# RMS norm of batches 1 to 8 on one compact tile, its inverse root spread by fp32r halves, and x reloaded into its own slot

## The chip, the cores and the metric

The kernel runs on one core of one Trainium2 chip. A core has TensorE (PE in the profile; PEld is its weight load), VectorE (DVE), ScalarE (ACT), GpSimd (POOL) and SyncE (SP, which only issues DMAs here). Each engine works through its own list of instructions in order and waits on semaphores for the others. The metric is the device time of one execution in microseconds, as the median of several runs.

## The reference

Three layers in a row: a linear attention with an RMS norm over each head's 64 values, a maximum of three projections with an output projection, and a second FFN with a squared ReLU.

```python
# q, k, v: 8 batches, 8 heads, 576 rows, 64 columns
kv = np.einsum('bhsd,bhse->bhde', k, v)
out = np.einsum('bhsd,bhde->bhse', q, kv)
rms = np.sqrt(np.mean(out * out, axis=-1, keepdims=True) + 1e-06)
x = out / rms * g_norm                  # -> 4608 tokens x 512
h = np.maximum(np.maximum(x @ w1, x @ w2), x @ w3)   # 512 -> 768
x = h @ w_out                                        # 768 -> 512
r = np.maximum(x @ w_in, 0.0)                        # 512 -> 2048
out = (s * (r * r) + b) @ moe2_w_out                 # 2048 -> 512
```

## The kernel before

**Tiles.** A token block is 512 tokens. Each batch has 576 rows: 512 make block 0 to 7, and the 64 left over of all batches make block 8. The attention output `o` of a batch is kept with features on the partitions: four tiles of 128 x 512, one for each pair of heads p (two heads of 64 features). So the mean of the squares of a head is a sum over 64 partitions, which TensorE makes by a product with a constant matrix, and the factor 1/rms must be on all those partitions again before VectorE can multiply.

**Number form.** Products are in fp32r, a reduced form of fp32. An fp32 value is kept as two of them: a high part (ScalarE copies and rounds, `hi_part`) and a low part (a subtraction, `lo_part`). `mm3` (lines 160 to 163) makes one product as three: hi x hi, hi x lo, lo x hi. Some small products are in plain fp32; the profile shows each of those as two MATMUL instructions.

**Stages.** For j = 0 to 4, `g1_part` makes 18 groups (3 projections x 6 blocks of 128) of 12 products each from x, and `g2_mm` then makes 4 output blocks of 18 products from h. These two fill TensorE; the attention of later batches is woven between their groups. x of batches 0 and 1 stays on chip. From batch 2 on the normed o is stored to DRAM (`xd`) and, for batches 2 to 4, loaded again before its turn. Batches 5 to 8 are read from `xd` in a later stage. From about 380 us on there is no attention left.

**Order.** Every piece of work is a `job` with a place in time, an engine, a cost and the names that it reads, writes and allocates. `arrange` (lines 71 to 131) goes through the jobs with these costs and writes a fixed order for each engine: an engine takes the earliest planned job that is ready. So a job that gets other costs or another place moves its neighbours too. The engines then follow that order, whatever the real durations are.

**Three ways to norm.** `PLAIN` = 2 divides the batches.

- Batch 0: compact, two head pairs at a time. `msc_mm` multiplies the squares with `means` (128 x 32) in fp32 and puts pair p on partitions 32p to 32p + 31 of one PSUM tile, each by a tile of its own of the array (128 rows, 32 columns). `rsqrt_c` makes Ln, Exp, Square on ScalarE and two steps on VectorE for all of them at once, with the result in `uc`. `bc_mm` spreads a pair of rows over 128 partitions by a product of `spread` with `uc`, 32 rows and 128 columns of the array, in fp32. `normed` multiplies o with it.
- Batch 1: the same with all four head pairs in one tile (`WIDE` = 4).
- Batches 2 to 8: each head pair alone on a whole tile. The square is split in two fp32r halves (`sq_hi` on VectorE or ScalarE, `sq_lo` on GpSimd), `ms_mm` makes two products of 128 x 128 x 512 with `ones`, whose result stands on all partitions already, and `rsqrt` and `newton` make three steps on ScalarE and three on VectorE for each pair. Batch 8 squares `o_rem`, the left-over rows.

**Buffers.** PSUM tile `o` (two banks, one buffer) holds the attention output of two head pairs, and in batches 0 and 1 also `bc`. PSUM tile `ms` (one bank) holds the left-over rows of the attention product and the means. `xh` and `xl` hold x of one block, one buffer each. `x_back` (line 533) loads x of a batch by head pair into small tiles, of which there are two: the first two quarters are loaded early, the last two when the first have been read. It is issued on SP's queue, as nearly all DMAs are.

Of the kernel before, what the change touches and what calls it, by code (L numbers as in the profile page):

```python
# [30 lines left out]
def attention_max_ffn_relu2_ffn(ctx: ExitStack, tc, q, k, v, g_norm, w1, w2, w3, wo, wi, w2o, s, b, out):  # L31
# [462 lines left out]

    def normed(bb, p):
        o = st["o", bb, p]
        stt(out=o, in0=o, scalar=g_sb, in1=st["bc", p // 2][p % 2], op0=ALU.mult, op1=ALU.mult)

    def rsqrt(bb, p, n):
        if n == 0:  # L500
            st["y", p] = at_.tile([P, N], F32, tag="y", name=f"y_{bb}_{p}")
            act(out=st["y", p], in_=st["ms", p], func=AF.Ln, bias=eps)
        elif n == 1:
            act(out=st["y", p], in_=st["y", p], func=AF.Exp, scale=-0.5)
        else:
            st["u", p] = at_.tile([P, N], F32, tag="u", name=f"u_{bb}_{p}")
            act(out=st["u", p], in_=st["y", p], func=AF.Square)

    def newton(bb, p, n):
        y, u = st["y", p], st["u", p]  # L510
        if n == 0:
            stt(out=u, in0=st["ms", p], scalar=EPS, in1=u, op0=ALU.add, op1=ALU.mult)
        elif n == 1:
            stt(out=u, in0=u, scalar=-3.0, in1=y, op0=ALU.add, op1=ALU.mult)
        else:
            o = st["o", bb, p]
            stt(out=o, in0=o, scalar=g_sb, in1=u, op0=ALU.mult, op1=ALU.mult)
# [1066 lines left out]
```

## Time and profile before

| | us |
|---|---|
| median of 3 runs | 1358.96 (1358.86 to 1359.13) |
| profiled execution | 1358.27 |
| its span, first to last instruction | 1356.5 |
| TensorE busy | 1336.8 |
| VectorE busy | 982.4 |
| ScalarE busy | 788.0 |
| GpSimd busy | 68.1 |

The profile shows one execution. An instruction's row has its start, its duration, the line of the kernel and the tiles. Durations on TensorE overlap: a product is in flight for 0.39 us while the next one starts 0.23 us behind it. What a product costs is therefore the distance from one start to the next. Where an engine stood idle before an instruction, brackets say how long and what it waited for.

### The profile page before, as it was taken

What the parts mean: (1) busy time and instruction counts of PE and PEld (TensorE: products, weight loads), DVE (VectorE), ACT (ScalarE), POOL (GpSimd) and SP (SyncE); (2) the same over time, 40 slices, a digit from 0 to 9 for tenths busy, and PEclk for the clock granted to TensorE, in tenths of its full rate; (3) what the DMA queues carried; (4) which work ended last, traced back from release to release, by engine and by line L of the source; (5) the groups of instructions that cost most, each with busy time, mean ns of one, the idle gap of its engine ahead of it and who ended that gap; (6) DMA issues with size and microseconds to landing.
All of it is one profiled execution on the core that took longest, in us unless ns stands there. A gap on an engine that the chain in (4) does not pass through costs nothing.

```text
span 1356.5 us, 19727 instructions
## 1 busy us (share of the span) xinstructions
PE 1336.8 (99%) x6948; PEld 1102.0 (81%) x6948; DVE 982.4 (72%) x1671; ACT 788.0 (58%) x1399; POOL 68.1 (5%) x58
## 2 busy tenths in 40 slices
PE   7999999999999999999999999999999999999998
PEld 4777777778888888878888889888888888888888
DVE  4994666767658885477647768658888888888875
ACT  6873555556435453165546567567775656566565
POOL 0001212123110000000000000000000000000000
PEclk9999999999999999999999999999999999999999
DMA  9988988753527638575535645436584464554531
GB/s 267 298 181 210 221 215 224 209 157 95 152 87 249 240 117 267 205 244 184 177 149 196 238 174 169 172 139 223 194 307 151 142 211 142 178 164 138 182 113 48
DMA packets 241010, 251.81 MB, mean 186 GB/s; under 512 B 119184, under 2 KB 177552, under 8 KB 238736
## 3 DMA queue, kind: packets, MB, share of 16 engines
q1 hardware_dynamic: 240752, 250.31, 59.9%
q8 instruction: 54, 0.88, 0.3%
q14 instruction: 44, 0.36, 0.1%
q10 hardware_dynamic: 160, 0.26, 0.1%
HBM read 149.85 MB, written 100.66 MB: 185 GB/s over the span
## 4 chain that ended last, share of the span: by engine, by line
PE 95%; DVE 2%; DMA 1%; SPq 1%; ACT 1%; issue 0%; ACTq 0%; DVEq 0%
PE ps_a L999 15%; PE zs_a L1153 14%; PE g L161 10%; PE g L163 9%; PE g L162 9%; PE ps_b L999 7%; PE fp_a L1392 7%; PE zs_b L1153 7%; PE zs_c L1153 4%; PE ps_c L999 4%; PE fp_b L1392 4%; PE fp_c L1392 2%; PE kvor L348 1%; PE ops L417 1%; PE ms L456 1%; DMA vrem<-in_v_dram 1%
## 5 line engine op out<-in xcount | busy, mean ns | idle before, releaser
L290 ACT ACTIVATE zx<-z 128x512 fp32r<-128x512 f32 (+1 forms) x280 | 158.4, 586 | 122.6 <-PE zs_a L1153 37.8
L1153 PE MATMUL zs_a<-zx,w_q 128*128 128x512 f32 (+1 forms) x960 | 210.9, 368 | 1.0 <-DVE zx L293 1.0
L293 DVE TENSOR_TENSOR zx<-z,zx 128x512 fp32r<-128x512 f32 (+1 forms) x280 | 171.3, 634 | 53.6 <-ACT zx L290 50.2
L999 PE MATMUL ps_a<-x_q,w_q 128*128 128x512 f32 (+1 forms) x960 | 206.0, 368 | 0.0
L1153 PEld LDWEIGHTS zs_a<-zx,w_q 128*128 128x128 f32 x960 | 168.2, 189 | 31.2 <-DVE zx L293 1.2
L999 PEld LDWEIGHTS ps_a<-x_q,w_q 128*128 128x128 f32 x960 | 167.8, 189 | 29.9
L161 PE MATMUL g<-xh,w_w 128*128 128x512 f32 x360 | 142.6, 396 | 0.0
L163 PE MATMUL g<-xh,w_w 128*128 128x512 f32 x360 | 140.4, 390 | 0.7 <-DVE w_w L293 0.7
L162 PE MATMUL g<-xl,w_w 128*128 128x512 f32 x360 | 140.3, 390 | 0.0
L1153 PE MATMUL zs_b<-zx,w_q 128*128 128x512 f32 (+1 forms) x480 | 108.5, 368 | 1.9 <-DVE zx L293 1.9
L999 PE MATMUL ps_b<-x_q,w_q 128*128 128x512 f32 (+1 forms) x480 | 105.1, 368 | 0.0
L1153 PEld LDWEIGHTS zs_b<-zx,w_q 128*128 128x128 f32 x480 | 84.5, 188 | 17.3 <-DVE zx L293 2.3
L999 PEld LDWEIGHTS ps_b<-x_q,w_q 128*128 128x128 f32 x480 | 84.2, 189 | 15.0
L161 PEld LDWEIGHTS g<-xh,w_w 128*128 128x128 f32 x360 | 67.5, 188 | 15.6 <-issue 0.8
L163 PEld LDWEIGHTS g<-xh,w_w 128*128 128x128 f32 x360 | 67.6, 188 | 15.5 <-DVE w_w L293 1.1
L162 PEld LDWEIGHTS g<-xl,w_w 128*128 128x128 f32 x360 | 67.6, 188 | 13.7 <-DVE xl L293 0.3
L576 DVE TENSOR_TENSOR h<-g,h 128x512 f32<-128x512 f32 x60 | 41.5, 691 | 38.5 <-PE g L163 37.3
L1028 ACT ACTIVATE cs<-cs 128x512 f32<-128x512 f32 (+1 forms) x60 | 35.1, 586 | 53.5 <-DVE cs L855 52.8
L1400 ACT ACTIVATE fc<-fp_a 128x512 f32<-128x512 f32 x36 | 21.4, 597 | 68.4 <-PE fp_a L1392 66.0
L1015 ACT ACTIVATE cs<-ps_a 128x512 f32<-128x512 f32 (+1 forms) x80 | 43.4, 555 | 24.9 <-PE ps_a L999 21.0
L1153 PE MATMUL zs_c<-zx,w_q 128*128 128x512 f32 (+1 forms) x240 | 54.1, 368 | 0.0
L855 DVE TENSOR_TENSOR cs<-ps_b,cs 128x512 f32<-128x512 f32 (+1 forms) x40 | 24.9, 637 | 39.5 <-issue 32.5
(325 smaller groups left out, 2498.9 us busy)
## 6 DMA issues: line engine op xcount, KB each, us to landing
z<-gd SPq DMA_DIRECT2D x64, 512.0 KB
gd<-cs SPq DMA_DIRECT2D x96, 256.0 KB
z<-gd SPq DMA_DIRECT2D x48, 256.0 KB
x1d<-x SPq DMA_DIRECT2D x36, 256.0 KB
sd<-fs SPq DMA_DIRECT2D x18, 512.0 KB
raw_w<-in_moe_w_dram SPq DMA_DIRECT2D x18, 511.0 KB
k<-in_k_dram SPq DMA_DIRECT2D x32, 256.0 KB
v<-in_v_dram SPq DMA_DIRECT2D x32, 256.0 KB
```

Of the source, the lines that this page charges most:

```text
L161: nc.tensor.matmul(ps, lhsT=w[:, 0, sl], rhs=xh, start=first, stop=False)
L162: nc.tensor.matmul(ps, lhsT=w[:, 0, sl], rhs=xl, start=False, stop=False)
L163: nc.tensor.matmul(ps, lhsT=w[:, 1, sl], rhs=xh, start=False, stop=last)
L290: act(out=out, in_=src, func=AF.Copy)
L293: eng.tensor_tensor(out=out, in0=src, in1=hi.bitcast(F32), op=ALU.subtract)
L576: nc.vector.tensor_tensor(out=st["h", m], in0=ps, in1=st["h", m], op=ALU.max)
L855: eng.tensor_tensor(out=out, in0=in0, in1=in1, op=op)
L999: nc.tensor.matmul(ps, lhsT=w[:, a, c], rhs=x[:, b_], start=new and k == 0 and e == 0, stop=k == HK - 1 and e == 2, skip_group_check=True)
L1015: act(out=st["cs", G, i, m], in_=st["ps", G, BANK[i], m][:, :n], func=AF.Copy)
L1028: act(out=h, in_=st["ps", G, BANK[i], m][:, :width(q)] if i == 6 else h, func=AF.Relu)
L1153: nc.tensor.matmul(ps, lhsT=w[:, a, c], rhs=x[:, b_], start=new and k_ == 0 and e == 0, stop=k_ == 3 and e == 2, skip_group_check=True)
L1392: nc.tensor.matmul(ps, lhsT=w[:, u, c], rhs=x[:, v_], start=new and k == 0 and e == 0, stop=k == HK - 1 and e == 2, skip_group_check=True)
```

## The change

Batches 1 to 8 are normed in one way, by the new `plan_wide`. The four squares of a batch go through one `msc_mm` of four fp32 products and one `rsqrt_c` on a 128 x 512 tile. Its result `uc` is split in two fp32r halves, `uh` and `ul`, and `wide_bc` spreads a pair by four fp32r products on two row groups of 32 (both head pairs' high halves, then both low halves) into PSUM tile `o`. `spread` becomes an fp32r tile; batch 0 reads it as fp32. `ones`, `sq_hi`, `sq_lo`, `ms_mm`, `rsqrt` and `newton` go.

x of batches 2 to 4 is loaded into the tile `xl` itself, as fp32, and split there: `xh` is its high part, and the low part overwrites it. All four quarters can be loaded only when the last product with the old `xl` is done. The DMAs are issued by ScalarE.

```diff
-    ones = at_.tile([P, P], F32R, name="ones")
-    nc.vector.tensor_copy(out=ones, in_=onesf)
...
-    spread = at_.tile([P, 2, D], F32, name="spread")
+    spread = at_.tile([P, 2, D], F32R, name="spread")
...
-    def sq_lo(bb, p):
-        st["sqhl", p].append(at_.tile([P, N], F32R, tag="sql", name=f"sql_{bb}_{p}"))
-        lo_part(st["sqhl", p][1], st["sq", p], st["sqhl", p][0], nc.gpsimd)
-
-    def ms_mm(bb, p):
-        ps = st["ms", p] = psa.tile([P, N], F32, tag="ms", name=f"ms_{bb}_{p}")
-        sqh, sql = st["sqhl", p]
-        nc.tensor.matmul(ps, lhsT=ones, rhs=sqh, start=True, stop=False)
-        nc.tensor.matmul(ps, lhsT=ones, rhs=sql, start=False, stop=True)
+    def u_hi(bb, eng):
+        t = st["uh"] = at_.tile([P, N], F32R, tag="y", name=f"uh_{bb}")
+        if eng == "ACT":
+            act(out=t, in_=st["uc"], func=AF.Copy)
+        else:
+            ts(out=t, in0=st["uc"], scalar1=1.0, scalar2=None, op0=ALU.mult)
+
+    def u_lo(bb):
+        st["ul"] = at_.tile([P, N], F32R, tag="xb", name=f"ul_{bb}")
+        lo_part(st["ul"], st["uc"], st["uh"], nc.vector)
+
+    def wide_bc(bb, p):
+        t = st["bc", p // 2] = psa.tile([P, 2, N], F32, tag="o", name=f"bc_{bb}_{p}")
+        for e, nm in enumerate(("uh", "ul")):
+            for i in range(2):
+                sl = slice(32 * (p + i), 32 * (p + i + 1))
+                nc.tensor.matmul(t[:, i], lhsT=spread[sl].rearrange("p h d -> p (h d)"), rhs=st[nm][sl],
+                                 start=e == 0, stop=e == 1, tile_position=(32 * (p + i), 0))
...
+    def x_tiles(j):
+        if j not in xs:
+            xs[j] = (base.tile([P, KD, N], F32R, tag="xh", name=f"xh_{j}"),
+                     base.tile([P, KD, N], F32R, tag="xl", name=f"xl_{j}"))
+        return xs[j]
+
     def x_back(bb, c):
-        t = st["o", bb, 2 * (c % 2) + c // 2] = at_.tile([P, N], F32, tag=XB[c % 2], name=f"xb_{bb}_{c}")
-        nc.sync.dma_start(out=t, in_=xd[bb][:, c])
-
-    def plan_x_back(bb, pos, x):
+        t = st["o", bb, 2 * (c % 2) + c // 2] = x_tiles(bb)[1][:, 2 * (c % 2) + c // 2].bitcast(F32)
+        nc.scalar.dma_start(out=t, in_=xd[bb][:, c])
+
+    def plan_x_back(bb, x):
         for c in range(KD):
-            nm, at = f"xb{bb}.{c}", x + 0.1 * c
-            job(pos + 0.01 * c if c < 2 else at, "SP", 1.1, x_back, bb, c, r=[f"xd{bb}:{c}"], w=[nm], a=[(XB[c % 2], nm)], lag=3.0)
-            plan_x(bb, 2 * (c % 2) + c // 2, at + 0.05, [nm], "DVE", c == 0)
+            p, at = 2 * (c % 2) + c // 2, x + 0.1 * c
+            job(at, "ACT", 0.6, x_back, bb, c, r=[f"xd{bb}:{c}"], w=[f"xl{bb}:{p}"], a=[("xh", f"xh{bb}"), ("xl", f"xl{bb}")] if c == 0 else [], lag=3.0)
+            plan_x(bb, p, at + 0.05, [f"xl{bb}:{p}"], "DVE", False)
...
+    def plan_wide(bb, t, f, sq):
+        o = [[f"or{p}:{b_}" for b_ in range(B)] if bb == B else [f"o{bb}.{p // 2}:{p % 2}"] for p in range(NP)]
...
+        job(t, "PE", 1.1, msc_mm, bb, 0, NP, r=[f"sq{bb}.{p}" for p in range(NP)], w=[ms], a=[("ms", ms)])
+        for i in range(5):
+            job(t + f * (0.3 + 0.1 * i), "DVE" if i > 2 else "ACT", 0.7 if i > 2 else 0.65, rsqrt_c, bb, 0, NP, i,
+                r=[[ms], [y], [y], [ms], [y]][i], w=[[y], [y], [uc], [uc], [uc]][i], a=[("y", y), ("u", uc)] if i == 0 else [])
+        job(t + 0.9 * f, "DVE/ACT", (0.42, 0.6), u_hi, bb, r=[uc], w=[uh], a=[("y", uh)])
+        job(t + 1.0 * f, "DVE", 0.69, u_lo, bb, r=[uc, uh], w=[ul], a=[("xb", ul)])
+        for k in range(0, NP, 2):
+            b = f"bc{bb}.{k // 2}"
+            job(t + f * (1.3 + 0.3 * k), "PE", 0.5, wide_bc, bb, k, r=[uh, ul], w=[f"{b}:{k}", f"{b}:{k + 1}"], a=[("ops", b)])
+            for p in (k, k + 1):
+                job(t + f * (1.6 + 0.3 * k), "DVE", 0.7, normed, bb, p, r=[f"{b}:{p}", "g_sb"], w=o[p])
...
-    PLAIN, ROWS, QP = 2, 1, 1
+    ROWS, QP = 1, 1
+    FN, F1, ZB = 1, 1, 4
...
+        if bb == 1:
+            plan_wide(bb, A1 + AS + 4.7, F1, lambda p: A1 + AS * (p // 2) + 3.75 + 0.3 * (p % 2))
+        else:
+            plan_wide(bb, t + 10.7 * FA, FN, lambda p: t + FA * (6 * (p // 2) + 3.75 + 0.3 * (p % 2)))
```

Three places show how the engines' lists move. In the names, `g1_3_17` is group 17 of the first FFN for block j = 3, `ms_7_3` and `bc_7_2` belong to batch 7 and head pair 3 or 2, and the last number only tells buffers apart.

TensorE at the end of the first FFN of block 3, before: the old mean product of batch 7, head pair 3, between two groups.

```order
L163 MATMUL g1_3_16_3335<-xh_3_2679,w_w_16_897 128x512
L456 MATMUL ms_7_3_3355<-sqh_7_3_3323,ones_134 128x512
L457 MATMUL ms_7_3_3355<-sql_7_3_3328,ones_134 128x512
L161 MATMUL g1_3_17_3359<-xh_3_2679,w_w_17_905 128x512
L162 MATMUL g1_3_17_3359<-xl_3_2680,w_w_17_905 128x512
```

The same place now, one group later: behind the last group stand the second spread of batch 7 (two products with `uh`, two with `ul`) and the four products of batch 8's mean.

```order
L163 MATMUL g1_3_17_3178<-xh_3_2547,w_w_17_910 128x512
L451 MATMUL bc_7_2_3201<-uh_7_3149,spread_140 128x512 x2
L451 MATMUL bc_7_2_3201<-ul_7_3168,spread_140 128x512 x2
L458 MATMUL msc_8_3210<-sq_8_0_3120,means_130 32x512
L458 MATMUL msc_8_3210<-sq_8_1_3123,means_130 32x512
L458 MATMUL msc_8_3210<-sq_8_2_3140,means_130 32x512
L458 MATMUL msc_8_3210<-sq_8_3_3146,means_130 32x512
L161 MATMUL g2_3_0_3220<-h_3_0_2814,w_o_0_948 128x512
```

A batch had four pairs of `ms` and now has one row of four `msc` and two rows of `bc`; in every other batch the FFN's groups stand between them.

VectorE while the first weights are converted, before: the stretch that ends with `qt_1_3`, the transposed q that the second attention product of batch 1 needs.

```order
L293 TENSOR_TENSOR w_w_12_795<-tr_w12_743,w_w_12_795 128x512
L275 SCALAR_TENSOR_TENSOR tr_w13_775<-tr_w13_775 128x512
L264 SCALAR_TENSOR_TENSOR tr_w14_798<-raw_w14_713,tr_w14_798 128x512
L293 TENSOR_TENSOR h_0_2_805<-h_0_2_735,h_0_2_805 128x512
L293 TENSOR_TENSOR w_w_13_808<-tr_w13_775,w_w_13_808 128x512
L275 SCALAR_TENSOR_TENSOR tr_w14_798<-tr_w14_798 128x512
L252 TENSOR_SCALAR gc_w16_822<-raw_w16_746 128x512
L404 STREAM_TRANSPOSE qt_1_3_826<-qraw_1_516 128x576
```

The same stretch now.

```order
L286 TENSOR_TENSOR w_w_12_792<-tr_w12_740,w_w_12_792 128x512
L270 TENSOR_TENSOR tr_w13_769<-tr_w13_769 128x512
L268 SCALAR_TENSOR_TENSOR tr_w14_772<-tr_w14_772 128x512
L554 TENSOR_TENSOR h_0_2_729<-g1_0_8_687,h_0_2_729 128x512
L286 TENSOR_TENSOR w_w_13_806<-tr_w13_769,w_w_13_806 128x512
L286 TENSOR_TENSOR w_w_14_811<-tr_w14_772,w_w_14_811 128x512
L286 TENSOR_TENSOR h_0_2_814<-h_0_2_729,h_0_2_814 128x512
L257 SCALAR_TENSOR_TENSOR tr_w15_803<-raw_w15_727,tr_w15_803 128x512
L397 STREAM_TRANSPOSE qt_1_3_826<-qraw_1_510 128x576
```

Counted from the `gc_w` of weight tile 12 (at 59.59 us in the trace of before), 17 instructions stood ahead of `qt_1_3` and 19 stand there now.

ScalarE between the first FFN of block 3 and that of block 4, before: x of batch 4 comes from the small tiles `xb`, and the norm of batch 8 goes pair by pair.

```order
L290 ACTIVATE xh_4_3401<-xb_4_0_2944 128x512
L270 ACTIVATE tr_p17_3380<-tr_p17_3380,lim_70 128x512
L290 ACTIVATE h_3_5_3406<-h_3_5_3349 128x512
L258 ACTIVATE tr_p17_3380<-raw_p17_3299,lim_70 128x512
L434 ACTIVATE sq_8_1_3413<-o_rem_152 128x512
L290 ACTIVATE xh_4_3401<-xb_4_1_2965 128x512
L502 ACTIVATE y_8_0_3437<-ms_8_0_3416,eps_64 128x512
```

The same place now: ScalarE issues the loads of x itself, and their splitting stands between the steps of batch 8's one chain (`yc_8`, `uc_8`, `uh_8`).

```order
L516 DMA xl_4_3207<-xd4_95 128x512 x2
L283 ACTIVATE h_3_5_3218<-h_3_5_3164 128x512
L468 ACTIVATE yc_8_3237<-msc_8_3210,eps_64 128x512
L516 DMA xl_4_3207<-xd4_95 128x512
L470 ACTIVATE yc_8_3237<-yc_8_3237 128x512
L283 ACTIVATE xh_4_3206<-xl_4_3207 128x512
L472 ACTIVATE uc_8_3238<-yc_8_3237 128x512
L283 ACTIVATE xh_4_3206<-xl_4_3207 128x512
L243 ACTIVATE tr_p18_3265<-raw_p18_3192 128x512
L283 ACTIVATE xh_4_3206<-xl_4_3207 128x512
L263 ACTIVATE tr_p18_3265<-tr_p18_3265,lim_70 128x512
L438 ACTIVATE uh_8_3272<-uc_8_3238 128x512
```

The last quarter's load stands directly behind `uh_8`, and its `xh` behind the copies of the first two output blocks.

## Rows read from the trace of the kernel before

**Rows 1.** The page's busy table: us, share of the span, instructions.
```profile
PE 1336.8 (99%) x6948; PEld 1102.0 (81%) x6948; DVE 982.4 (72%) x1671; ACT 788.0 (58%) x1399; POOL 68.1 (5%) x58
```
**Rows 2.** Windows: stretch, length, then busy us (instructions) of each engine, clock, DMA.
```profile
100.00:150.00 50.00, 50.00 (x320) 39.36 (x319) 26.68 (x47) 21.54 (x37) 9.03 (x7) 1.00 0.84 220
...
300.00:350.00 50.00, 50.00 (x232) 40.70 (x231) 34.20 (x52) 32.56 (x55) 14.09 (x10) 1.00 0.42 127
350.00:400.00 50.00, 50.00 (x222) 41.40 (x221) 27.19 (x41) 19.21 (x31) 7.95 (x6) 1.00 0.36 114
```
**Rows 3.** TensorE's waits from 30 us: whom, us in total, times, longest.
```profile
PE ops L417 <- DVE qt L404: 0.7, 1, 0.7
PE g L163 <- DVE w_w L293: 0.7, 1, 0.7
```
**Rows 4.** Timeline of TensorE, batch 2: start, duration, line, tiles, count [idle before].
```profile
122.11 0.39 PE L162 MATMUL g<-xl,w_w 128*128 128x512 f32 x1
122.34 0.39 PE L163 MATMUL g<-xh,w_w 128*128 128x512 f32 x1
122.57 0.39 PE L456 MATMUL ms<-sqh,ones 128*128 128x512 f32 x1
...
123.02 0.39 PE L161 MATMUL g<-xh,w_w 128*128 128x512 f32 x1
```
**Rows 5.** Timeline of TensorE, batch 1's mean.
```profile
81.86 0.39 PE L163 MATMUL g<-xh,w_w 128*128 128x512 f32 x1
82.18 1.06 PE L463 MATMUL msc<-sq,means 128*32 128x512 f32 x8
83.17 0.50 PE L161 MATMUL g<-xh,w_w 128*128 128x512 f32 x1
...
86.03 0.39 PE L161 MATMUL g<-xh,w_w 128*128 128x512 f32 x1
```
**Rows 6.** Timeline of TensorE, batch 1's first spread.
```profile
91.25 0.39 PE L163 MATMUL g<-h,w_o 128*128 128x512 f32 x1
91.56 1.13 PE L492 MATMUL bc<-uc,spread 32*128 32x512 f32 x4
92.62 0.50 PE L161 MATMUL g<-h,w_o 128*128 128x512 f32 x1
...
93.89 0.39 PE L163 MATMUL g<-h,w_o 128*128 128x512 f32 x1
```
**Rows 7.** Lines 463 and 492 on TensorE: duration in ns (min/median/max), first and last.
```profile
L463 PE MATMUL msc<-sq,means x16: 592/605/617, 19.3 to 82.7; 128*32 128x512 f32 x16
...
L492 PE MATMUL bc<-uc,spread x16: 587/640/692, 24.9 to 96.1; 32*128 32x512 f32 x16
```
**Rows 8.** Timeline of TensorE, second attention product of batch 1.
```profile
68.14 1.07 PE L417 MATMUL ops<-qt,kvc 64*64 64x512 f32 x2
69.95 0.65 PE L417 MATMUL ops<-qt,kvc 64*64 64x512 f32 x3 [0.74 <-DVE qt L404]
```
**Rows 9.** Timeline of VectorE ahead of that product.
```profile
59.59 0.42 DVE L252 TENSOR_SCALAR gc_w<-raw_w 128x512 uint16<-128x512 uint16 x1
...
69.11 0.78 DVE L404 STREAM_TRANSPOSE qt<-qraw 128x576 f32<-128x576 f32 x1
```
**Rows 10.** Steps of the old chain: duration in ns (min/median/max), first and last.
```profile
L502 ACT ACTIVATE y<-ms,eps x28: 667/689/695, 123.3 to 358.3; 128x512 f32<-128x512 f32 x28
...
L512 DVE SCALAR_TENSOR_TENSOR u<-ms,u x28: 677/691/693, 125.3 to 360.7; 128x512 f32<-128x512 f32 x28
```
**Rows 11.** Timelines of SP and ScalarE: last quarter of x of batch 4.
```profile
338.99 0.37 SPq L535 DMA_DIRECT2D xb<-xd  x1
...
343.80 0.63 ACT L290 ACTIVATE xh<-xb 128x512 fp32r<-128x512 f32 x1 [2.72 <-DMA xb<-xd]
```
**Rows 12.** Timeline of TensorE: second FFN of block 3, first FFN of block 4.
```profile
331.67 0.39 PE L161 MATMUL g<-h,w_o 128*128 128x512 f32 x1
...
348.89 0.39 PE L161 MATMUL g<-xh,w_w 128*128 128x512 f32 x1
```

More of the change, by code (lines that the diff above doesn't have):

```diff
@@ L432, in o_sq @@
     def o_sq(bb, p, src):
-        sq = st["sq", p] = at_.tile([P, N], F32, tag=SQ[p] if bb < PLAIN else "sq", name=f"sq_{bb}_{p}")
+        sq = st["sq", p] = at_.tile([P, N], F32, tag=SQ[p], name=f"sq_{bb}_{p}")
         act(out=sq, in_=src, func=AF.Square)
@@ L491, in bc_mm @@
             sl = slice(32 * (p + i), 32 * (p + i + 1))
-            nc.tensor.matmul(t[i], lhsT=spread[sl].rearrange("p h d -> p (h d)"), rhs=st["uc"][sl],
+            nc.tensor.matmul(t[i], lhsT=spread[sl].bitcast(F32).rearrange("p h d -> p (h d)"), rhs=st["uc"][sl],
                              start=True, stop=True, tile_position=(32 * (p + i), 0))
     def normed(bb, p):
[L496 to L517, printed above, removed]
+        o, bc = st["o", bb, p], st["bc", p // 2]
+        stt(out=o, in0=o, scalar=g_sb, in1=bc[p % 2] if isinstance(bc, list) else bc[:, p % 2], op0=ALU.mult, op1=ALU.mult)
     xs = {}
@@ L548, in x_hi @@
     def x_hi(j, p):
-        if j not in xs:
-            xs[j] = (base.tile([P, KD, N], F32R, tag="xh", name=f"xh_{j}"),
-                     base.tile([P, KD, N], F32R, tag="xl", name=f"xl_{j}"))
-        hi_part(xs[j][0][:, p], st["o", j, p])
+        hi_part(x_tiles(j)[0][:, p], st["o", j, p])
     def x_lo(j, p, eng):
@@ L681, in plan_compact @@
                     w=[f"o{bb}.{k // 2}:{k % 2}"])
-        if bb < 2:
-            plan_x(bb, p, x, o, "DVE", p == 0)
-        else:
-            plan_x_out(bb, p, t + 7.2 * u, o)
+        plan_x(bb, p, x, o, "DVE", p == 0)
     def plan_norm(bb, p, t, u, x, eng):
-        sq, ms, y, uu = (f"{c}{bb}.{p}" for c in ("sq", "ms", "y", "u"))
-        if bb < B:
-            o = [f"o{bb}.{p // 2}:{p % 2}"]
-            src = lambda: st["ops", p // 2][:, p % 2]
-            r = [f"ops{bb}.{p // 2}:{i}" for i in (p // 2 * 2, p // 2 * 2 + 1)]
-        else:
-            o = r = [f"or{p}:{b_}" for b_ in range(B)]
-            src = lambda: o_rem[:, p, :]
@@ L707, in plan_norm @@
-        job(t + 3.3 * u, "PE", 0.46, ms_mm, bb, p, w=[ms], a=[("ms", ms)], r=["h" + sq, "l" + sq])
-        for n in range(3):
-            job(t + (4 + 0.3 * n) * u, "ACT", 0.65, rsqrt, bb, p, n, r=[(ms, y, y)[n]], w=[(y, y, uu)[n]],
-                a=[[("y", y)], [], [("u", uu)]][n])
-        for n in range(3):
-            job(t + (6 + 0.3 * n) * u, "DVE", 0.7, newton, bb, p, n, r=[[ms], [y], [uu, "g_sb"]][n], w=[[uu], [uu], o][n])
-        plan_x_out(bb, p, t + 7.2 * u, o)
+        o = [f"o{bb}.{p // 2}:{p % 2}"]
@@ new lines, in plan_norm @@
+        r = [f"ops{bb}.{p // 2}:{i}" for i in (p // 2 * 2, p // 2 * 2 + 1)]
+        job(t, "ACT", 0.59, lambda: o_sq(bb, p, st["ops", p // 2][:, p % 2]), r=r, w=[f"sq{bb}.{p}"], a=[(SQ[p], f"sq{bb}.{p}")])
+        plan_compact(bb, p, t, u, x, eng, o, f"sq{bb}.{p}")
+    def plan_wide(bb, t, f, sq):
+        o = [[f"or{p}:{b_}" for b_ in range(B)] if bb == B else [f"o{bb}.{p // 2}:{p % 2}"] for p in range(NP)]
+        ms, y, uc, uh, ul = (f"{c}c{bb}" for c in ("ms", "y", "u", "uh", "ul"))
+        for p in range(NP):
+            src, r = (lambda p=p: st["ops", p // 2][:, p % 2]), [f"ops{bb}.{p // 2}:{i}" for i in (p // 2 * 2, p // 2 * 2 + 1)]
+            if bb == B:
+                src, r = (lambda p=p: o_rem[:, p]), o[p]
+            job(sq(p), "ACT", 0.59, lambda p=p, src=src: o_sq(bb, p, src()), r=r, w=[f"sq{bb}.{p}"], a=[(SQ[p], f"sq{bb}.{p}")])
+        job(t, "PE", 1.1, msc_mm, bb, 0, NP, r=[f"sq{bb}.{p}" for p in range(NP)], w=[ms], a=[("ms", ms)])
[10 more added lines that the diff above has]
+                if bb == 1:
+                    plan_x(bb, p, 20 + 0.1 * p, o[p], "DVE", p == 0)
+                else:
+                    plan_x_out(bb, p, t + f * (1.9 + 0.3 * k), o[p])
@@ L782, in attention_max_ffn_relu2_ffn @@
             for p in range(NP):
[L783 removed]
+                st["o", B, p] = o_rem[:, p]
+            plan_wide(B, t + ZB * FA, FN, lambda p: t + (ZB - 1) * FA + 0.1 * p)
             break
```

29 lines of the change are left out of this document (3 added, 26 removed).

## The prediction

> **What bounds the kernel now.** I read the busy table first: TensorE is busy 1336.8 of 1356.5 us, VectorE 72% [rows 1]. Then the stages: from 100 us to 400 us, where the norms of batches 2 to 8 lie, each 50 us stretch holds 50.00 us of TensorE at a granted clock of 1.00, the higher of its two levels (2.4 GHz) [rows 2]. Then TensorE's waits: between 30 and 560 us the list has only two, 0.7 us on `w_w` among the first weights and 0.7 us on `qt` at 69 us [rows 3]. So here the end is set by how much TensorE is given to do; time taken off ScalarE, VectorE or GpSimd is worth nothing unless a TensorE wait hangs on it, and there are almost none to give back. A product of 512 columns costs one step: 222 of them fill the 50 us from 350 on (0.225 us), and one stands 0.227 us behind the other here [rows 2, 4].
>
> **Removed: the 28 old mean products.** Batches 2 to 8 do four pairs of `ms` each. Both run in the same form as the FFN's products: from the product ahead at 122.34 to the one behind at 123.02 is 0.68 us, less one ordinary step 0.453 [rows 4]. 28 x 0.453 = **-12.7 us**. With them go 28 hi parts, 28 GpSimd low parts, and on ScalarE and VectorE 12 steps each a batch become 3 and 6, plus the two halves of u. None of that is on TensorE's path: worth 0.
>
> **Added: the compact mean.** The trace has it, for batch 1: four fp32 products with 32 columns of output, side by side. From 81.86 to 86.03 is 4.17 us and holds 13 ordinary steps (2.95); the four cost 1.22 us [rows 5]. 7 x 1.22 = **+8.5 us**.
>
> **Added: the spread by fp32r halves.** The nearest row is batch 1's fp32 spread of a pair: from 91.25 to 93.89 is 2.64 us with 6 ordinary steps (1.36), so 1.28 us [rows 6]. It is four instructions. One fp32 instruction lasts 0.605 to 0.640 us against 0.39 for an fp32r product, some 0.22 longer, so it streams about 0.44 us [rows 4, 7]. Four in a row would be 1.76; since all took 1.28, the two row groups ran side by side: 2 x 0.44 = 0.88, and 0.40 is toll for leaving the ordinary form and coming back (the first product behind lasts 0.50, not 0.39). The mean gives 1.22 - 0.88 = 0.34 for it. No row shows fp32r on row groups. Four instructions of 0.227 in two groups are 0.45; that is the low end, without any toll. The high end is four in a row with toll, 4 x 0.227 + 0.40 = 1.30, about what fp32 costs. I take 0.45 + 0.39 = 0.84, since every excursion in the trace pays the toll. 14 x 0.84 = **+11.8 us**; batch 1 exchanges two pairs, 2 x (0.84 - 1.28) = **-0.9 us**.
>
> All tolls in the trace are at places that are both fp32 and split, so rows can't tell which of the two is charged. The Trainium skill, TensorEngine Tiling, Key Properties, says that a change of tiling mode drains TensorE; by that rule fp32r on row groups pays as well, and the pair is 0.84, not 0.45, a difference of 6.2 us over 16 pairs. No run here shows it yet.
>
> **Moved on TensorE.** In batch 8 the mean stands directly behind a spread, which saves one toll (-0.4). In batch 1 the four kv blocks stood around one spread; now two of them stand alone between products, two more excursions (+0.8 at most, by the toll). Together **+0.4 us**.
>
> **Moved on VectorE, batch 1.** TensorE's second attention product of batch 1 stood 0.74 us waiting for `qt` of head pair 3 [rows 8]. VectorE came to it at 69.11, 17 instructions after the one at 59.59: 9.52 us without idle time [rows 9]. The mean of batch 1 is now planned one group earlier, the list shifts, and 19 instructions stand in that stretch. At 0.56 us each, the mean of the 17, that is 10.6 us, so TensorE waits 1.1 us more; no later wait is there to swallow it. **+1.1 us** (0 if the two extra ones find an idle place ahead, 2 if VectorE has to wait for ScalarE on top).
>
> **New waits.** TensorE now waits for a chain: four squares, mean, three ScalarE and four VectorE steps, spread. A step on a whole tile lasts 0.69 [rows 10], so from mean to spread the chain is at most 4.8 us without hand-overs. The shortest distance between them on TensorE, in batch 6, holds 24 products (5.4 us) and one kv block; the other batches have 24 with four kv blocks or more. So 0 there, with up to 1 us in a batch if something stands in front. In batch 8 the chain shares ScalarE with the reload of x, below.
>
> **The reload.** Four DMAs move from SP's queue to ScalarE's and can only start when the FFN's last product with the old x is done. In before the last quarter landed 4.8 us after its issue [rows 11]. What hides it is the second FFN product, 17.2 us for j = 3 [rows 12]. With T the end of the last first-FFN product: issued T + 0.4, landed T + 5.2, then `xh` and `xl`; the fourth quarter is issued behind `uh`, at about T + 10, and is ready at T + 16.5, wanted at T + 21. Worth 0 for x itself. But `xh` stands between the Exp and the Square of batch 8, and a second wait of this kind ahead of `uh`: by these numbers `ul` ends at T + 10.3 and TensorE comes to the spread at T + 10.2. I take **+0.4 us**, 0 to 2 (a us for each us that landing takes longer). Fewer SP transfers gain nothing: no TensorE wait hangs on them.
>
> **The sum.** -12.7 + 8.5 + 11.8 - 0.9 + 0.4 + 1.1 + 0.4 = **+8.6 us**. The profiled execution took 1358.27 us, of which 1356.5 are the span; the median is 1358.96. On the median: **1367.6 us**, 0.63% slower. With the low spread: 16 x 0.39 = 6.2 less, +2.4. With the high one: 16 x 0.46 = 7.4 more, +16.0.
>
> **Rivals.**
>
> *No toll for fp32r (not slower).* If the toll belongs to fp32 and not to the split, a pair costs 0.45. For it: the old fp32r pair paid nothing [rows 4]. Against: its tile was whole. It gives 1361.4, and 1360 if the two small waits don't come either. It decides below 0.47 us a pair: there the sum falls under 2.7 us, the 0.2% that a measurement of this kernel can tell from no change. The Trainium skill, TensorE: Matmul & The Clock Gate, Part 3, gives this result: tiles in different row groups start some 4 ns apart and together last about one product. By that rule a pair is two such spans, 0.45, and the time 1361.4; the fp32 pair above ran side by side as the rule says, but cost 0.40 more.
>
> *Row groups one after another.* 1.30 a pair: 1375. Against: the fp32 pairs of the same shape overlapped [rows 6].
>
> *A late chain.* If ScalarE or VectorE hold a link for a us in each of the eight batches, TensorE stands: up to +8, 1375. For: in four batches the mean stands only 12 products (2.7 us) behind the product that feeds the copy and the last two squares. Against: VectorE has room in these stages, and the old chain, with GpSimd in it, never made TensorE wait.
>
> *Something is gained.* Only if TensorE's work shrinks after all: a pair at 0.45, means cheaper in series than the one measured, and the wait on `qt` gone. Some 1355; nothing in the profile speaks for it.
>
> **How the numbers follow.** Forecast with toll 0.60 (1363 to 1372 by its own terms); no toll 0.18; one after another 0.08; late chain 0.10; gain 0.04. Slower by over 0.2% is the forecast, the two slow rivals: 0.78. Within 0.2%: nearly all of the no-toll case, 0.17. Faster: 0.05. The range, **1360.5 to 1374**, takes in the no-toll case and leaves the tops of the two slow ones and the gain outside.
>
> **What will show it.** In the profile after: the step over a `bc` pair in the second FFN batch (0.84; 0.45 or 1.30 for the rivals); the mean at 1.22 in every batch; TensorE's wait on `qt` near 2 us; no wait of TensorE on `xl`; at most a few tenths on `ul` in batch 8; and the last stages, from 450 us, shifted as a block by the sum. I am wrong if a TensorE wait of more than 2 us appears that is not named here, or if the early stages end sooner than before.

## The result, and the profile after

The changed kernel takes **1368.97 us** (median of 4 runs, 1367.31 to 1370.16) against 1358.91 for the kernel before (1358.42 to 1359.13, 4 runs): a ratio of **1.0078**, 95% interval 1.0066 to 1.0091. It is slower, by 10.1 us on the medians; the prediction was 1367.6 with 1360.5 to 1374.0. The profiled execution is the longest of the four, 1370.16 us, with a span of 1368.1.

An excursion is in this text a stretch of TensorE's products on row or column groups of the array between ordinary ones, and its toll is what it costs beyond the streaming of its own products. The spread pair, which no row of before showed, is here. Timeline of TensorE in the changed kernel, batch 2, first spread (start, duration, line, tiles, count):

```profile
144.91 0.39 PE L163 MATMUL g<-xh,w_w 128*128 128x512 f32 x1
145.23 0.49 PE L451 MATMUL bc<-uh,spread 32*128 32x512 f32 x2
145.57 0.39 PE L451 MATMUL bc<-ul,spread 32*128 32x512 f32 x2
145.89 0.50 PE L161 MATMUL g<-xh,w_w 128*128 128x512 f32 x1
146.22 0.40 PE L162 MATMUL g<-xl,w_w 128*128 128x512 f32 x1
```

From the product ahead to the one behind is 0.98 us, less one ordinary step 0.75; and the step from that product to the next is 0.33, 0.11 more than an ordinary one (it lasts 0.50, as in [rows 6]). Together that is **0.86 us a pair**, where 0.84 was forecast. The four products start at two times, not at four: both row groups run side by side. The step is the same to 0.01 in the other eleven pairs that stand alone in batches 2 to 8.

The mean in the same view, batch 2: 1.31 less 0.23 is 1.08, and 0.11 behind, **1.19 us**, as batch 1's in [rows 5].

```profile
135.54 0.39 PE L163 MATMUL g<-xh,w_w 128*128 128x512 f32 x1
135.86 1.07 PE L458 MATMUL msc<-sq,means 128*32 128x512 f32 x8
136.85 0.50 PE L161 MATMUL g<-xh,w_w 128*128 128x512 f32 x1
137.19 0.39 PE L162 MATMUL g<-xl,w_w 128*128 128x512 f32 x1
```

TensorE's waits in the changed kernel (whom, us in total, times, longest), the one that answers to [rows 3] and a new one:

```profile
PE ops L410 <- DVE qt L397: 2.2, 2, 2.0
...
PE kvor L341 <- DVE o_rem L433: 0.4, 1, 0.4
```

The wait on `qt` has grown from 0.74 [rows 8] to 2.00 us. The two rows left out, 0.5 us on `v` and 0.2 on `w_w` near 36 us, stand in the place of the 0.7 on `w_w` of [rows 3]: the FFN's products behind them are as late as ahead of them. No wait on `xl` or `ul` is in the list, and none of over 2 us that the prediction did not name. What it did not foresee stands right behind that wait. Timeline of TensorE, second attention product of batch 1 and the FFN products behind it:

```profile
72.08 0.65 PE L410 MATMUL ops<-qt,kvc 64*64 64x512 f32 x3 [2.00 <-DVE qt L397]
...
73.94 0.63 PE L163 MATMUL g<-xh,w_w 128*128 128x512 f32 x1
74.37 0.63 PE L161 MATMUL g<-xh,w_w 128*128 128x512 f32 x1
```

The products last 0.63 and start 0.43 us apart instead of 0.227. The windows of the same stretch (busy us and instructions of each engine, then the granted clock, here 0.85, 0.80 and, in the single us from 74 on, 0.50) say why:

```profile
70.00:75.00 5.00, 3.00 (x20) 1.98 (x20) 5.00 (x10) 5.00 (x9) 0.00 (x0) 0.85 0.66 210
75.00:80.00 5.00, 5.00 (x20) 3.98 (x19) 5.00 (x10) 5.00 (x11) 0.00 (x0) 0.80 0.91 180
...
74.00:75.00 1.00, 1.00 (x4) 0.81 (x3) 1.00 (x3) 1.00 (x2) 0.00 (x0) 0.50 0.56 197
```

For eight products TensorE runs at the lower of its two levels, 1.2 GHz; their steps are longer by 0.17 to 0.21 us, 1.55 us in all. The clock falls 1.5 us behind the end of the wait. In before the clock is 1.00 in every stretch of 5 us from 60 to 85.

**Where the 11 us of this execution lie.** The start of the n-th FFN product in the one trace less that in the other gives the delay at each point. It is 0.1 us at the first (28.8 us), 0.9 ahead of the second attention product of batch 1, 2.1 behind it, 3.7 when the clock is back, still 3.7 behind the last spread of batch 1, 11.9 behind batch 8, and 11.1 at the last matmul. So 3.6 us are gathered up to the end of batch 1 and 8.2 in batches 2 to 8; in the later stages 0.8 are won back, where a wait on `zx` is 0.2 us instead of 1.0.

### The profile page after: what moved, and what is told of

It reads as the page before. It is cut to its first block, busy times and chain, and to the rows that moved or that the text cites. A ratio compares the mean times of both kernels' runs of the same rounds, so it can differ in the third digit from the quotient of the medians.

```text
span 1368.1 us, 19646 instructions
## 1 busy us (share of the span) xinstructions
PE 1348.2 (99%) x7004; PEld 1098.1 (80%) x7004; DVE 948.7 (69%) x1625; ACT 742.7 (54%) x1324; POOL 29.8 (2%) x30
## 4 chain that ended last, share of the span: by engine, by line
PE 93%; SPq 2%; DVE 2%; DMA 2%; ACT 0%; issue 0%; ACTq 0%; DVEq 0%
PE ps_a L975 14%; PE zs_a L1129 14%; PE g L161 9%; PE g L163 9%; PE g L162 9%; PE ps_b L975 7%; PE fp_a L1368 7%; PE zs_b L1129 7%; PE ps_c L975 4%; PE fp_b L1368 4%; PE zs_c L1129 4%; PE fp_c L1368 2%; PE kvor L341 1%; PE ops L410 1%; SPq L356 1%; PE bc L451 1%
## 5 line engine op out<-in xcount | busy, mean ns | idle before, releaser
L161 PE MATMUL g<-xh,w_w 128*128 128x512 f32 x360 | 144.8, 402 | 0.0
L163 PE MATMUL g<-xh,w_w 128*128 128x512 f32 x360 | 141.3, 392 | 0.2 <-DVE w_w L286 0.2
L283 ACT ACTIVATE h<-h 128x512 fp32r<-128x512 f32 x30 | 19.0, 633 | 89.4 <-DVE h L554 89.4
```

The source lines that it names most:

```text
L161: nc.tensor.matmul(ps, lhsT=w[:, 0, sl], rhs=xh, start=first, stop=False)
L163: nc.tensor.matmul(ps, lhsT=w[:, 1, sl], rhs=xh, start=False, stop=last)
L283: act(out=out, in_=src, func=AF.Copy)
```

## The experiments

All are timed beside runs of the kernel before in three groups, each on one chip: `spread_twice`, `spread_whole`, `batch1_old` and `squares_late` (before: median 1358.77, 8 runs); `qt_later`, `reload_only`, `one_late` and `best` (1357.99, 30 runs); `spread_fp32`, `mean_twice` and `best_reload` (1358.41, 15 runs). The expected times start from 1358.8 or from the changed kernel's 1369.0, so a ratio compares better than a time. Edits are against the changed kernel unless said.

**1. Is the toll the split's?** The first edit doubles the work inside an excursion, the second does the same sums without row groups.

```
-        for e, nm in enumerate(("uh", "ul")):
+        for e, nm in enumerate(("uh", "ul", "uh", "ul")):
...
-                                 start=e == 0, stop=e == 1, tile_position=...)
+                                 start=e % 2 == 0, stop=e % 2 == 1, tile_position=...)
```

> The changed kernel with every fp32r spread pair computed twice in the same excursion (8 instructions instead of 4, the second time over the first, same result). Theory (two row groups side by side, 0.45, plus a toll of about 0.41 for each excursion): 0.45 more a pair, step 1.31, 16 x 0.45 = 7.3, time 1376.3. Rival one (row groups one after another, no toll, 4 x 0.227 = 0.91): 0.91 more, 14.5, time 1383.5. Rival two (every step inside a split excursion takes 0.33): 0.66 more, 10.6, time 1379.5.

Measured 1375.53 us (ratio 1.0119, 1.0103 to 1.0135). Timeline of TensorE, batch 2's second spread:

```profile
148.34 0.39 PE L163 MATMUL g<-xh,w_w 128*128 128x512 f32 x1
148.66 0.50 PE L451 MATMUL bc<-uh,spread 32*128 32x512 f32 x2
148.99 0.39 PE L451 MATMUL bc<-ul,spread 32*128 32x512 f32 x2
149.23 0.39 PE L451 MATMUL bc<-uh,spread 32*128 32x512 f32 x2
149.46 0.39 PE L451 MATMUL bc<-ul,spread 32*128 32x512 f32 x2
149.78 0.50 PE L161 MATMUL g<-xh,w_w 128*128 128x512 f32 x1
```

The inner starts are 0.23 us apart, two products each time; going in, the first step inside, and coming out are each some 0.1 longer. The excursion costs 1.21 and 0.11 behind, 1.32: four products more cost 0.46, not 0.91 and not 0.66. The two rivals, row groups one after another and 0.33 for every step, are ruled out.

```
-        for e, nm in enumerate(("uh", "ul")):
-            for i in range(2):
-                sl = slice(32 * (p + i), 32 * (p + i + 1))
-                nc.tensor.matmul(t[:, i], lhsT=spread[sl]..., rhs=st[nm][sl], ..., tile_position=...)
+        for i in range(2):
+            for e, nm in enumerate(("uh", "ul")):
+                nc.tensor.matmul(t[:, i], lhsT=whole[:, p + i], rhs=st[nm], start=e == 0, stop=e == 1)
```

`whole` holds, for each head pair, the weights of `spread` in its 32 rows and zeros in the other 96. `ul` moves to another buffer.

> The changed kernel with the spread on the whole array: the weights padded with zeros to 128 rows, four fp32r products of 128 rows a pair, no row groups; every engine's order as in the changed kernel. Theory (the toll belongs to the split): 4 x 0.227 = 0.91 a pair against 0.86, the first product behind lasts 0.39 and not 0.50, 16 x 0.05 = 0.8 more, time 1369.8. Rival (any excursion from the stream of FFN products pays the toll): 1.31 a pair, 7.2 more, 1376.

Measured 1370.48 us (1.0083, 1.0067 to 1.0098). Same place, same view:

```profile
149.15 0.40 PE L163 MATMUL g<-xh,w_w 128*128 128x512 f32 x1
149.39 0.39 PE L457 MATMUL bc<-uh,whole 128*128 128x512 f32 x1
149.62 0.39 PE L457 MATMUL bc<-ul,whole 128*128 128x512 f32 x1
...
150.07 0.40 PE L457 MATMUL bc<-ul,whole 128*128 128x512 f32 x1
150.31 0.39 PE L161 MATMUL g<-xh,w_w 128*128 128x512 f32 x1
```

Every step is 0.23 to 0.24, the product behind lasts 0.39: 0.93 a pair and no toll. The toll belongs to the row groups, and it eats most of what they save: 0.86 with them, 0.93 without.

**2. fp32 against fp32r, and the mean.**

```
-        for e, nm in enumerate(("uh", "ul")): ...
+        for i in range(2):
+            nc.tensor.matmul(t[:, i], lhsT=spread[sl].bitcast(F32)..., rhs=st["uc"][sl], start=True, stop=True, ...)
```

> The changed kernel with the spread of batches 1 to 8 done as in batch 1 of the kernel before, two fp32 products a pair on row groups, all other engines' work unchanged (the two halves are still made, and not read). Theory (same toll, 0.88 of streaming against 0.45): 1.25 a pair against 0.86, 16 x 0.39 = 6.2 more, time 1375.2. Rival (fp32 costs less where fewer instructions stand in the excursion): under 1.0 a pair, 1371.

Measured 1374.96 us (1.0122, 1.0107 to 1.0138); timeline of TensorE, batch 2's first spread:

```profile
143.04 0.39 PE L163 MATMUL g<-xh,w_w 128*128 128x512 f32 x1
143.36 1.13 PE L450 MATMUL bc<-uc,spread 32*128 32x512 f32 x4
144.42 0.50 PE L161 MATMUL g<-xh,w_w 128*128 128x512 f32 x1
```

1.38 less 0.23, and 0.11 behind: 1.26 a pair. The halves save 0.40 a pair of TensorE's time against fp32.

```
-        for p in range(p0, p0 + n):
+        for p in [*range(p0, p0 + n)] * (2 if bb else 1):
             nc.tensor.matmul(st["msc"][32 * p:32 * (p + 1)], lhsT=means, ...)
```

> The changed kernel with the compact mean of batches 1 to 8 computed twice in the same excursion (eight fp32 products of 32 columns instead of four, same result). Theory (two at a time side by side at 0.44, plus a toll of 0.31 for the excursion): 0.88 more a mean, step 2.07 against 1.19, 8 x 0.88 = 7.0, time 1376.0. Rival one (all four side by side, the rest of 1.19 is toll): 0.44 more, 3.5, time 1372.5. Rival two (no toll, 1.19 is all streaming): 1.19 more, 9.5, time 1378.5.

Measured 1376.7 us (1.0133, 1.0119 to 1.0146); batch 2's mean:

```profile
136.74 0.39 PE L163 MATMUL g<-xh,w_w 128*128 128x512 f32 x1
137.06 1.92 PE L458 MATMUL msc<-sq,means 128*32 128x512 f32 x16
138.91 0.50 PE L161 MATMUL g<-xh,w_w 128*128 128x512 f32 x1
```

1.94 and 0.11 behind, 2.05 against 1.19: 0.86 for four more products. So four such products stream in 0.86, two at a time, and of the mean's 1.19 some 0.33 is toll; both rivals (0.44 and 1.19 more) are ruled out. The time is 0.7 above the expected one; its four runs lie 5 us apart (1373.82 to 1378.75).

**3. Batch 1: the wait on qt.** The first kernel undoes the norm of batch 1, the second only the planned place of its squares.

```
         if bb == 1:
-            plan_wide(bb, A1 + AS + 4.7, F1, lambda p: A1 + AS * (p // 2) + 3.75 + 0.3 * (p % 2))
+            for p in range(NP):
+                plan_norm(bb, p, A1 + AS * (p // 2) + 3.9 + 0.5 * (p % 2), 0.2, 20 + 0.1 * p, "DVE")
```

> The changed kernel with the norm of batch 1 planned and computed as in the kernel before (fp32 spread, squares at their old places); batches 2 to 8 and the reload stay changed. Theory (the first 3.7 us of the difference come from batch 1, through TensorE's wait on qt and the low clock that follows it): the second attention product of batch 1 waits 0.7 us instead of 2.0, the granted clock stays at 1.00 from 65 to 80 us, the time is about 11.6 - 3.7 = 7.9 us above before, 1366.8. Rival (later stages swallow what is lost early): still 1369.

Measured 1366.73 us (1.0056, 1.0041 to 1.0071). The wait is 0.7, the clock 1.00 from 60 to 85 us.

```
-            plan_wide(bb, A1 + AS + 4.7, F1, lambda p: A1 + AS * (p // 2) + 3.75 + 0.3 * (p % 2))
+            plan_wide(bb, A1 + AS + 4.7, F1, lambda p: A1 + AS * (p // 2) + 3.9 + 0.5 * (p % 2))
```

> The changed kernel, but the four squares of batch 1 planned 0.15 and 0.35 position units later, where the kernel before had them; VectorE's order up to the transpose of qt for head pair 3 is then that of before. Theory (the place of the squares on ScalarE shifts weight-conversion steps to VectorE ahead of qt): wait on qt back to 0.7, no low clock, batch 1's own excursions as in the changed kernel (6.2 us), time 1366.8. Rival (the new chain of batch 1 itself makes TensorE late): wait stays 2.0 and the time 1369.

Measured 1365.59 us (1.0049, 1.0034 to 1.0063). Timeline of TensorE:

```profile
70.28 0.65 PE L410 MATMUL ops<-qt,kvc 64*64 64x512 f32 x3 [0.74 <-DVE qt L397]
...
71.74 0.40 PE L162 MATMUL g<-xl,w_w 128*128 128x512 f32 x1
```

The wait and the clock are those of before, and the FFN products behind the second attention product of batch 1 start 0.3 us after those of before, no more than at the first product, instead of 3.7. Two numbers of the plan, a shift of 0.15 and 0.35 position units for the four squares on ScalarE, decide all of it. The rival is ruled out: the chain of batch 1 itself costs nothing there. The ratio of this kernel is 0.0029 under the changed kernel's, some 3.9 us, with intervals that no longer meet.

**4. Does the wait make the clock fall?** Here the edit is to the kernel before.

```
-        nc.vector.transpose(t, st["qraw"][:, p].rearrange("p i f -> p (i f)"))
+        for _ in range(3 if (bb, p) == (1, 3) else 1):
+            nc.vector.transpose(t, st["qraw"][:, p].rearrange("p i f -> p (i f)"))
```

> The kernel before with one thing added: VectorE transposes qt of batch 1's head pair 3 three times instead of once (same result), 2 x 0.70 us more ahead of TensorE's second attention product of batch 1. Nothing of the norm or the reload is changed. Theory (a wait of 2 us there is what makes the granted clock fall for the next 3 to 4 us): wait 0.74 + 1.40 = 2.1 us, the granted clock falls below 1.00 between 68 and 78 us as in the changed kernel, time 1.4 us for the wait and some 1.5 to 2 for the clock above before: 1361.9. Rival (the low clock comes with the changed order of the other engines or with the new products): wait 2.1, clock 1.00, 1.4 above before: 1360.2. Second rival (the list after it has room): no difference, 1358.8.

Measured 1360.57 us (11 runs, 1359.39 to 1363.62; ratio 1.0022, 1.0014 to 1.0031). Timeline and windows of the profiled execution:

```profile
70.67 0.65 PE L418 MATMUL ops<-qt,kvc 64*64 64x512 f32 x3 [2.35 <-DVE qt L405]
...
73.10 0.63 PE L163 MATMUL g<-xh,w_w 128*128 128x512 f32 x1
```

```profile
70.00:75.00 5.00, 4.33 (x21) 2.94 (x22) 5.00 (x9) 3.40 (x7) 0.00 (x0) 0.66 0.34 106
```

With nothing of the norm changed, the longer wait brings the lower clock along in this execution. The wait grew by 1.61 us, and the kernel lost 2.6 us on the medians, by the interval 1.9 to 4.2: more than the wait. The two runs whose mean clock is 1.000 take 1359.39 and 1359.91 (1.4 and 1.9 above before, about the wait alone), the two at 0.997 take 1362.52 and 1363.62; for these runs there is no trace to say where the clock fell. It does not follow every time: in the profiled execution of `spread_fp32` the wait is 1.96 us, and the products behind it are at full speed:

```profile
71.05 0.65 PE L410 MATMUL ops<-qt,kvc 64*64 64x512 f32 x3 [1.96 <-DVE qt L397]
...
72.51 0.40 PE L162 MATMUL g<-xl,w_w 128*128 128x512 f32 x1
```

Of the six profiled executions with a wait of 1.9 us or more at this place (the changed kernel, `spread_twice`, `spread_whole`, `mean_twice`, `qt_later` and this one) the clock fell in the other five; of the seven with 0.7 to 0.95 us, in none. A second place, which no experiment aimed at, shows the same. Near the end of every execution TensorE waits for `zx`: behind 1.37 to 1.50 us, in eleven of the thirteen, the clock stayed at 1.00; behind 1.83 us in `qt_later` it stayed too; behind 1.81 us in `best` it fell:

```profile
1314.82 1.59 PE L1191 MATMUL zs_b<-zx,w_q 128*128 128x256 f32 x6 [1.81 <-DVE zx L311]
```

What decides between falling and not is open.

**5. The reload alone**, on the kernel before (the new `x_tiles`, `x_back` and `plan_x_back`; the old norm everywhere).

> The kernel before with only the reload of x changed: four DMAs a batch on ScalarE's queue into x's own slot, the old norm everywhere. Theory (the reload lies beside TensorE's second FFN product and costs nothing): within 0.1% of before, 1358.8, no TensorE wait on xl. Rival (ScalarE's waits for the landing delay batch 8's old mean chain or the next x): a TensorE wait on xl, ms or w of 1 to 3 us, 1360 to 1362. Second rival (fewer SP transfers help): 1 us or more faster.

Measured 1357.09 us (11 runs; ratio 0.9995, 0.9986 to 1.0004): no difference that these runs can tell. TensorE waits for nothing between 320 and 372 us.

**6. One product instead of four.** The whole-array form can do better than its four products for two head pairs: two more columns of `means` put the same mean into two more rows of each group, and a mask of one column keeps the high part in the first two rows and the low part in the next two. One product then adds both.

```
-        lo_part(st["ul"], st["uc"], st["uh"], nc.vector)
+        stt(out=st["ul"], in0=st["uc"], scalar=low, in1=st["uh"].bitcast(F32), op0=ALU.mult, op1=ALU.subtract)
...
+        for i in range(2):
+            nc.tensor.matmul(t[:, i], lhsT=whole[:, p + i], rhs=st["ul"], start=True, stop=True)
```

> The changed kernel with the squares of batch 1 at their old places (as in squares_late) and the spread of a head pair made by one product: the mean's weights fill two more rows of each group, a mask keeps the high part in the first two rows and the low part in the next two, and one whole fp32r product with padded weights adds both (two a pair of head pairs instead of four on row groups). Theory (each whole product costs 0.227 and no toll): 2 x 0.227 = 0.45 a pair against 0.86, 16 x 0.41 = 6.5 less than squares_late (1365.6), 1359.1, that is within 0.1% of before. Rival (whole products between others still cost the pair 0.86): 1365.6.

Measured 1361.87 us (1.0025, 1.0015 to 1.0036), 2.8 above the theory. A pair among ordinary products does cost 0.46, so the rival is ruled out. Two things were left out of the expectation. Pairs that stand beside other split work (in batch 1, batch 4 and batch 7) had shared its toll and save less: measured against `squares_late` product by product, the 14 pairs of batches 1 to 7 save 4.8 us, not 5.7. And in batch 8 the chain is now late, by 1.1 us. Against `squares_late` 6.5 us were expected, and the traces show 3.9 from the first FFN product to the last matmul; these two things hold 2.0 of the 2.6, and 0.6 goes in the later stages. TensorE and ScalarE in batch 8:

```profile
343.48 0.74 PE L467 MATMUL bc<-ul,whole 128*128 128x512 f32 x2 [0.84 <-DVE ul L462]
```

```profile
337.45 0.63 ACT L301 ACTIVATE xh<-xl 128x512 fp32r<-128x512 f32 x1 [1.70 <-DMA xl<-xd]
...
338.99 0.63 ACT L301 ACTIVATE xh<-xl 128x512 fp32r<-128x512 f32 x1 [0.38 <-DMA xl<-xd]
...
340.87 0.63 ACT L301 ACTIVATE xh<-xl 128x512 fp32r<-128x512 f32 x1 [0.69 <-DMA xl<-xd]
...
342.02 0.61 ACT L456 ACTIVATE uh<-uc 128x512 fp32r<-128x512 f32 x1
```

Three splittings of x, each waiting for its DMA, stand ahead of `uh`. That is the coupling of chain and reload that the prediction priced at 0 to 2. Counted from T, the end of the last first-FFN product, TensorE is done with the product ahead of the spread at T + 9.85, only 0.2 us earlier than in the changed kernel; the greater part is the chain, which ends at T + 10.8 instead of T + 10.0, because the second and third splitting wait 0.38 and 0.69 us for their loads instead of 0 and 0.25. Why the loads landed later was not tried.

**7. Towards something faster than both.** On the kernel before, only batch 1's spread in that one-product form; then the same with the new reload.

```
+            if bb == 1:
+                job(t + 5.3 * u, "DVE", 0.42, u_hi, bb, ...)
+                job(t + 5.4 * u, "DVE", 0.69, u_lo, bb, ...)
...
+                if k % 2 == 0 and bb == 1:
+                    job(t + 5.5 * u + 0.01 * k, "PE", 0.5, whole_bc, bb, k, r=["ul1", "whole:0"], ...)
```

> The kernel before with its old norm in batches 2 to 8 and its old reload; only batch 1's spread is made by one whole fp32r product a head pair (as in one_late) instead of fp32 on row groups. Theory: two pairs at 0.45 instead of 1.25, 1.6 us less, two VectorE steps more that nobody waits for: 1357.2 against 1358.8. Rival (the two VectorE steps or the moved order of batch 1 cost as much): 1358.8 or more.

Measured 1358.04 us (11 runs; ratio 1.0004, 0.9995 to 1.0013). The 1.6 us are not seen. In its trace the FFN products start 0.74 us earlier than in before already at 28.8 us, ahead of everything that batch 1 does, 0.52 behind the second attention product of batch 1 and 1.76 behind batch 1: its two pairs save 1.2 us, because the first stands between kv blocks (the five cost 3.48, four blocks alone 2.68 in batch 2 of before) and takes 0.80 there, not 0.46. Of the lead 0.90 is left at 367 us, since each of the 28 old mean pairs takes some 0.03 us more than in before, and 0.42 at the last matmul, behind the lower clock shown above. Why the old pairs are slower here is open; two of their rows, and the product behind:

```profile
120.58 0.39 PE L163 MATMUL g<-xh,w_w 128*128 128x512 f32 x1
120.81 0.40 PE L474 MATMUL ms<-sqh,ones 128*128 128x512 f32 x1
...
121.28 0.40 PE L161 MATMUL g<-xh,w_w 128*128 128x512 f32 x1
```

> The kernel before with both pieces that cost nothing or gained in their traces: batch 1's spread by one whole fp32r product a head pair, and the reload of x on ScalarE's queue; old norm in batches 2 to 8. Theory (the two small gains add, 1.5 us at 400 us of which half is lost in the later stages): 0.5 to 1.5 us under before, which these runs may or may not tell from no change. Rival (nothing of it reaches the end): within 0.3 us of before.

Measured 1357.47 us (11 runs; ratio 0.9993, 0.9984 to 1.0002). Its trace shows the same gain in batch 1, 1.26 us, and the same slower pairs. Neither can be told from the kernel before; by its interval the second may be 2.2 us faster or 0.3 slower.

## Why the prediction was right

The likeliest case came in, with its mechanism: each excursion pays a toll, also in fp32r. The old mean cost TensorE 1.81 us a batch in the form of the products around it; the new mean and two spreads leave that form three times a batch and cost 1.19 + 2 x 0.86 = 2.91. Term by term, in the profiled execution:

| Term | Predicted | Measured |
|---|---|---|
| 28 pairs of `ms` removed | -12.7 | -12.7 (28 x 0.453, none is left) |
| 7 compact means | +8.5 | +8.3 (1.19 each) |
| 14 spread pairs | +11.8 | +12.0 (0.86 each) |
| batch 1's two pairs | -0.9 | -0.8 (1.25 to 0.86) |
| kv blocks of batch 1 split, one toll shared | +0.4 | +0.5 |
| longer wait on `qt` | +1.1 | +1.3 |
| chain of batch 8 beside the reload | +0.4 | 0 |
| not in the sum: lower clock behind `qt` | 0 | +1.55 |
| not in the sum: wait on `o_rem`, batch 7 | 0 | +0.4 |

That is 10.55 of the 11.75 us gathered from the first FFN product to the end of batch 8. The rest: 0.8 us around the first attention product of batch 1, in this execution only (1.53 us from product to product in the four experiments with the same order there, 2.30 here); 0.3 in batches 2 to 8, where the ordinary steps between the excursions last 0.2282 us on the mean instead of 0.2275, 0.6 us in all, and the kv blocks, which the planner regrouped, cost some 0.3 less; and 0.1. `squares_late` is a second test of the sum: without the term for `qt` it gives 7.5 us, and that kernel, which has neither the longer wait nor the lower clock, took 6.8 more than before.

**The toll.** The decisive estimate was 0.45 + 0.39 a pair for a form that no row showed. That all tolls of before lay at places both fp32 and split left open which of the two was charged; `spread_whole` and `spread_fp32` answer it. The Trainium skill, TensorEngine Tiling, Key Properties, says that changing the tiling mode drains TensorE; the runs agree, at 0.41 us an excursion with fp32r, 0.38 with fp32 (1.26 less 0.88) and 0.33 for the column groups of the mean. The Trainium skill, TensorE: Matmul & The Clock Gate, Part 3, has tiles in different row groups run at once for about the time of one product; a pair estimated by it is 0.45. That holds inside an excursion (0.46 for four products more in `spread_twice`), but the section has no term for going in and out. That is where the no-toll rival failed.

**The moved blocks.** Batch 8's mean directly behind a spread saved 0.2, not 0.4: the two together cost 1.86 against 0.86 + 1.19, so two different splits next to each other still pay part. Timeline of TensorE in the changed kernel:

```profile
341.44 0.39 PE L163 MATMUL g<-xh,w_w 128*128 128x512 f32 x1
341.76 0.50 PE L451 MATMUL bc<-uh,spread 32*128 32x512 f32 x2
342.10 0.40 PE L451 MATMUL bc<-ul,spread 32*128 32x512 f32 x2
342.42 1.07 PE L458 MATMUL msc<-sq,means 128*32 128x512 f32 x8
343.42 0.50 PE L161 MATMUL g<-h,w_o 128*128 128x512 f32 x1
```

The kv blocks of batch 1 cost 0.7 more, against 0.8 at most in the forecast (all its excursions from the mean on, 6.32 us before and 6.24 now, of which the pairs saved 0.8).

**The wait on qt.** Size right, reason half right. VectorE needed 10.78 us from the `gc_w` of weight tile 12 to the transpose, against 10.6 forecast and 9.52 in [rows 9]. Timeline of VectorE in the changed kernel:

```profile
60.49 0.40 DVE L245 TENSOR_SCALAR gc_w<-raw_w 128x512 uint16<-128x512 uint16 x1
...
71.27 0.75 DVE L397 STREAM_TRANSPOSE qt<-qraw 128x576 f32<-128x576 f32 x1
```

But it is the squares' place on ScalarE that moved the list, not the mean's on TensorE, as `squares_late` shows. And the step failed to ask what a TensorE that stands still for 2 us does to its clock: that was worth as much as the longer wait itself, in five of the six profiled executions. It is the one mechanism that the prediction missed; the wait on `o_rem` is a small term beside it. Whether it is also why the runs of the changed kernel lie 2.9 us apart is not shown: the four runs of before lie 0.7 apart, but those beside the experiments up to 4.1.

**The reload and the chain.** Worth 0 for x, as forecast and as `reload_only` shows. The forecast had the first landing at T + 5.2 (T the end of the last first-FFN product, read as its start plus one step, 341.67) and `ul` at T + 10.3 against TensorE at T + 10.2; the rows give T + 5.0 for the `xh` that waited for it, T + 10.0 for `ul` and T + 10.1 for TensorE. The +0.4 was 0, by a margin of 0.14 us, and that is luck: the forecast put `ul` 0.1 behind TensorE. The shortest way from mean to spread is batch 6's, as the prediction says, but batches 7 and 8 have 36 products and no kv block there, not 24 with four; that changes nothing. Timelines of the changed kernel, all engines:

```profile
350.33 0.61 ACT L438 ACTIVATE uh<-uc 128x512 fp32r<-128x512 f32 x1
...
350.98 0.69 DVE L286 TENSOR_TENSOR ul<-uc,uh 128x512 fp32r<-128x512 f32 x1
...
351.81 0.49 PE L451 MATMUL bc<-uh,spread 32*128 32x512 f32 x2
```

The late-chain rival did not decide here; `one_late` is the kernel in which it does, in batch 8.

**The median** came out 1.4 us above the forecast. The missed terms, clock and `o_rem`, are 1.95 us where the clock falls, and the later stages won 0.8 back; that they partly cancel is luck.

## What to carry to other kernels

On a saturated TensorE count excursions as well as products: each change to row or column groups and back cost 0.33 to 0.41 us here, what one and a half to two ordinary products take, so short work on groups gains little over the same work on the whole array with zero-padded weights (0.86 against 0.93), and putting both halves of a split value into unused rows of one product beat both (0.46 among ordinary products, 0.80 between kv blocks). Work taken off ScalarE, VectorE and GpSimd was worth nothing where TensorE waited for none of it. When a planner places steps, a shift of 0.15 to 0.35 of a position can lengthen the one wait that matters, here from 0.7 to 2.0 us: look at the list of the engine that TensorE waits for, ahead of that wait.
